# Longformer attention into a squared-ReLU expert layer: value rows picked on TensorE, casts and memsets on GpSimd, one unit of matmuls moved

## The chip, the cores and the metric

The kernel runs on one core of one Trainium2 chip. The metric is the device time of one execution in microseconds (us). The span in a profile is about 1.8 us shorter than that time.

## The reference

Attention with a window of 32 and eight global tokens is computed for 8 batches of 8 heads over 576 tokens with head size 64. Its output goes as 4608 rows of 512 into an expert layer.

```python
def _attn_ref(q, k, v, global_idx):              # q, k, v: (8, 8, 576, 64) float32
    scores = 1/np.sqrt(64) * np.matmul(q, k.transpose(0, 1, 3, 2))
    mask = np.abs(pos[:, None] - pos[None, :]) <= 32
    mask = mask | is_global[:, None] | is_global[None, :]       # 8 global tokens
    ...                                          # softmax over the masked scores
    return np.matmul(attn, v)

def _moe_ref(x, w_in, w_out):                    # x: (4608, 512), d_ff 2048
    r = np.maximum(x @ w_in, 0.0)
    return (r * r) @ w_out
```

## The kernel before

A batch has four pairs of heads. "Outputs" multiplies a pair's weights `et` with the values `vb`, and "finish" normalises the result into `xT`, the input of the expert layer. A "scatter" puts the eight rows of the global tokens into `xT` as eight small VectorE copies. Their column numbers were loaded into VectorE registers from SBUF beforehand. A "unit" is four expert matmuls of 512 columns, and `take(n)` emits n units of a queue between pieces of attention. `keep_warm(n)` emits n filler matmuls on a zero tile.

Batch 0 (start of the program, shortened):

```python
def fetch_globals():                      # SyncE: row numbers from a register
    for g in range(NG):                   # batch 0's eight value rows, one DMA each
        nc.sync.dma_start(out=gv0[g : g + 1], in_=v[0, :, ds(at[g], 1), :]...)
    for nm in "kqv": ...                  # rows of batches 1 and 2: 24 more DMAs

tr_k(3, ...)                              # last transposes of batch 0
keep_warm(4)                              # fillers
half0(2)                                  # scores and exp of pair 2
columns()                                 # clamp the row numbers
masked(0, ets[1], WIN)
load_columns(0)                           # VectorE register load of the scatter columns
...
half0(3)
dve.tensor_copy(out=gv16, in_=gv0)        # cast of the value rows
spread_values(0, dve.tensor_copy)         # five copies into vb[0]
masked(0, ets[2], WIN); masked(0, ets[3], WIN)
half0_out(0, "mm"); half0_out(1, "sc"); half0_out(2, "acc"); half0_out(3, "mm")
...
scatter(0, 0)                             # then the first expert matmuls may start
...                                       # second half of batch 0, its scatter, expert work
```

Batch 1 (shortened; `unit` computes one pair and takes expert units in three places):

```python
for hp in range(NHP):
    unit(NHP + hp, SCHED["b1"][hp], ...)  # b1 = ((3,1,3), (2,1,2), (2,1,3), (2,1,3))
    if hp == 0:
        tokens_to_scratch(2)              # GpSimd: tokens of batch 2 to a DRAM scratch
        values(2)                         # GpSimd: value tiles of batch 2
    elif hp == 1:
        next_in_place()                   # VectorE: casts of batch 2's global rows
        globals_to_scratch(2)             # SyncE: those rows to the scratch
        transposes(2)                     # SyncE: kb, qb <- scratch, transposed loads
        value_globals(2)
    elif hp == 2:
        gather(0)
```

The softmax here doesn't subtract the row's maximum and nothing guards it: scores larger than these inputs give would overflow.

## Time and profile before

| | kernel before |
|---|---|
| Time, three runs | 327.07 us median (326.74 to 327.49) |
| Span of the profiled execution | 326.7 us (this execution took 328.47 us) |
| TensorE busy | 97% |
| TensorE without a gap from | 70.00 us to the last rows |

A timeline line reads: start in us, duration in us, engine, source line, operation, output<-input, shapes, count, and in brackets the idle time of that engine just before it and what ended it. PE is TensorE, DVE is VectorE, ACT is ScalarE, POOL is GpSimd, and SPq is SyncE's queue of transfers. First come batch 2's transposed loads in SyncE's queue, then the second scatter on VectorE.

```profile
57.84 3.07 SPq L421 DMA_TRANSPOSE kb<-scr_k  x1
61.15 2.51 SPq L421 DMA_TRANSPOSE qb<-scr_q  x1
```

```profile
35.94 1.66 DVE L741 COPY xT<-gx 128x4 f16 x8
```

```profile
64.88 0.41 ACT L692 ACTIVATE rec<-sc 128x288 f32<-128x288 f32 x1 [2.80 <-PE acc L660]
```

The entries of the two transposed loads in the queue last 5.58 us together and end at 63.66. The data of `qb` landed later, at 66.39, by the landing records of the packed trace. The eight scatter copies take 1.66 us, about 0.2 each. The logarithm is the first of the last pair of batch 1.

### The profile page before, as it was taken

How to read it: one execution, taken by the hardware profiler on the slowest of the kernel's cores; microseconds unless marked ns; L12 is line 12 of the kernel's file. 1: busy time of each engine (PE TensorE's matmuls, PEld its weight loads, DVE VectorE, ACT ScalarE, POOL GpSimd, SP SyncE). 2: the span in 40 equal slices, each digit the busy share in tenths (PEclk: the TensorE clock that was granted, in tenths of full speed). 3: DMA queues.
4: the chain of work that ended last, by engine and by line, in shares of the span. 5: the costliest groups of instructions: out<-in, count | busy, mean ns of one | idle time of the engine just before them, and what ended most of it. 6: DMA issues, size and time to landing. Idle time of an engine off the chain costs nothing.

```text
span 326.7 us, 6942 instructions
## 1 busy us (share of the span) xinstructions
PE 316.8 (97%) x2432; PEld 164.5 (50%) x2432; DVE 228.9 (70%) x684; ACT 211.7 (65%) x416; POOL 106.6 (33%) x138
## 2 busy tenths in 40 slices
PE   7979999999999999999999999999999999999996
PEld 3646774445554455455444554555455544444444
DVE  8686888687878875987598758885888674323421
ACT  4677985469953995499549954995499636404600
POOL 9734556309800870089107800680000000000000
PEclk9999999999999999999999999999999999999999
DMA  8999999949994999399969994999910011011012
GB/s 192 177 204 183 180 181 156 169 137 107 144 138 147 67 147 167 125 91 135 136 148 89 151 138 122 109 148 107 142 66 0 34 46 51 2 69 59 2 53 76
DMA packets 148356, 37.55 MB, mean 115 GB/s; under 512 B 136298, under 2 KB 143842, under 8 KB 148322
## 3 DMA queue, kind: packets, MB, share of 16 engines
q0 software_dynamic: 105168, 17.93, 76.2%
q1 hardware_dynamic: 43008, 19.05, 30.2%
q8 instruction: 19, 0.31, 0.4%
q14 instruction: 15, 0.12, 0.1%
q10 hardware_dynamic: 146, 0.13, 0.1%
HBM read 37.31 MB, written 17.05 MB: 166 GB/s over the span
## 4 chain that ended last, share of the span: by engine, by line
PE 80%; DVE 7%; SPq 6%; ACT 2%; issue 2%; DMA 1%; DVEq 0%
PE mm L577 26%; PE mm L514 26%; PE tr L514 9%; PE tr L577 7%; SPq L365 4%; PE sc L669 3%; PE acc L669 3%; PE sc L617 2%; SPq L360 2%; PE acc L617 2%; DMA grows<-in_v_dram 1%; DVE xT L741 1%; PE mm L533 1%; DVE gt L545 1%; DVE et L633 1%
## 5 line engine op out<-in xcount | busy, mean ns | idle before, releaser
L577 PE MATMUL mm<-w_out,gt 128*128 128x512 f16 x448 | 104.4, 379 | 0.0
L514 PE MATMUL mm<-xT,w_in 128*128 128x512 f16 x384 | 90.8, 379 | 0.4 <-DVE xT L741 0.4
L577 PEld LDWEIGHTS <-gt 128*128 128x128 f16 x560 | 52.4, 98 | 58.6
L514 PEld LDWEIGHTS <-w_in 128*128 128x128 f16 x512 | 47.5, 98 | 53.6 <-issue 0.6
L519 ACT ACTIVATE rl<-mm 128x512 f16<-128x512 f32 x96 | 54.5, 599 | 26.9 <-PE mm L514 26.9
L520 DVE TENSOR_TENSOR gt<-rl 128x512 f16<-128x512 f16 x128 | 51.1, 422 | 16.8 <-ACT rl L519 15.5
L626 ACT ACTIVATE et<-sc 128x880 f16<-128x880 f32 (+1 forms) x32 | 29.0, 905 | 44.3 <-PE sc L617 44.3
L633 DVE TENSOR_TENSOR et<-et,mask 128x880 f16<-128x880 f16 (+1 forms) x64 | 38.8, 614 | 21.9 <-ACT et L626 21.7
L113 POOL DMA_DIRECT2D vb<-in_v_dram x40 | 41.1, 1571 | 9.4 <-DMA w_in<-in_moe_w_in_dram 8.3
L514 PE MATMUL tr<-xT,w_in 128*128 128x512 f16 x128 | 33.0, 380 | 0.0
L554 DVE COPY ot<-mm 128x512 f32<-128x512 f32 (+1 forms) x29 | 19.6, 677 | 17.7 <-PE mm L577 15.8
L626 ACT ACTIVATE et<-acc 128x880 f16<-128x880 f32 (+1 forms) x32 | 29.1, 909 | 1.5 <-PE acc L617 1.4
L722 DVE TENSOR_TENSOR xT<-sc,rec 64x288 f16<-64x288 f32 (+1 forms) x55 | 25.1, 456 | 6.9 <-ACT rec L693 6.2
L693 ACT ACTIVATE rec<-rec 128x288 f32<-128x288 f32 x64 | 28.3, 443 | 2.0
L722 DVE TENSOR_TENSOR xT<-acc,rec 64x288 f16<-64x288 f32 (+1 forms) x55 | 25.0, 455 | 4.0 <-ACT rec L693 1.1
L409 POOL DMA_DIRECT2D scr_k<-in_k_dram x30 | 26.6, 1104 | 2.8 <-issue 2.8
L692 ACT ACTIVATE rec<-sc 64x288 f32<-64x288 f32 (+1 forms) x55 | 22.4, 406 | 7.7 <-PE sc L669 4.2
L917 POOL COPY pin<-gsh 1x1 f32<-1x1 f32 x5 | 0.9, 177 | 81.1 <-DVE gsh L710 81.1
L669 PEld LDWEIGHTS <-vb 128*128 128x128 f16 x288 | 21.3, 98 | 11.7 <-issue 0.3
L409 POOL DMA_DIRECT2D scr_q<-in_q_dram x24 | 24.7, 1563 | 3.3 <-DMA w_out<-in_moe_w_out_dram 3.3
L577 PE MATMUL tr<-w_out,gt 128*128 128x512 f16 x112 | 25.3, 379 | 0.0
L692 ACT ACTIVATE rec<-acc 64x288 f32<-64x288 f32 (+1 forms) x55 | 22.2, 403 | 1.2 <-PE acc L660 0.4
(143 smaller groups left out, 303.7 us busy)
## 6 DMA issues: line engine op xcount, KB each, us to landing
out_dram<-ot SPq DMA_DIRECT2D x35, 256.0 KB
vb<-in_v_dram POOLq DMA_DIRECT2D x32, 120.0 KB, 11.3
scr_q<-in_q_dram POOLq DMA_DIRECT2D x24, 144.0 KB, 5.7
scr_k<-in_k_dram POOLq DMA_DIRECT2D x24, 120.0 KB, 4.9
w_in<-in_moe_w_in_dram POOLq DMA_DIRECT2D x4, 512.0 KB, 9.5
w_out<-in_moe_w_out_dram POOLq DMA_DIRECT2D x4, 512.0 KB, 11.4
natk<-in_k_dram POOLq DMA_DIRECT2D x3, 288.0 KB, 15.2
natq<-in_q_dram POOLq DMA_DIRECT2D x3, 288.0 KB, 16.0
```

The costliest lines, as they stand in the source:

```text
L113: pool.dma_start(out=vb[b][NG : NG + KN[x], x, 2 * hs.start : 2 * hs.stop : 2], in_=v[b, hs, x * KT : x * KT + KN[x]].rearrange("h s d -> ...
L409: pool.dma_start(out=scr[(nm, b % 2)][x * pitch + off : x * pitch + off + hi - lo].rearrange("s (h d) -> s h d", d=D), in_=src[nm][b, :, l ...
L514: nc.tensor.matmul(ph, w_in[:, t, u * P : (u + 1) * P], xT[:, t, XOFF + c * TC : XOFF + (c + 1) * TC], start=(t == 0), stop=(t == NDM - 1),)
L519: nc.scalar.activation(out=rl, in_=ph, func=AF.Relu)
L520: nc.vector.tensor_tensor(out=gts[c][:, u, :], in0=rl, in1=rl, op=ALU.mult)
L577: nc.tensor.matmul(po, gts[c][:, f, m * P : (m + 1) * P], w_out[:, f, :], start=(f == 0), stop=(f == NFF - 1),)
L626: act.activation(out=et[:, :, 0:W], in_=sc[:, :, 0:W], func=AF.Exp, bias=0.0, scale=scale)
L633: dve.tensor_tensor(out=et[:, :, 0:W], in0=et[:, :, 0:W], in1=mask[:, MB[half] : MB[half] + W].unsqueeze(1).to_broadcast((P, 2, W)), op=AL ...
L669: nc.tensor.matmul(banks[e][:, o : o + w], vtf[:, t, vo : vo + P], et[:, e, so : so + w], start=(n == 0), stop=(n == nw - 1), skip_group_c ...
L692: act.activation(out=rec[r], in_=av[xs][rs, :, 0:GTOK], func=AF.Ln)
L693: act.activation(out=rec, in_=rec, func=AF.Exp, scale=-1.0)
L722: dve.tensor_tensor(out=xT[r, hp, x0 : x0 + HS].rearrange("p (k x) -> p k x", k=2), in0=av[x][r, :, 0:GTOK], in1=rec[r], op=ALU.mult,)
```

## The change

The intent is to take work off VectorE and SyncE on the way to the first expert matmuls, and off VectorE in batch 1. Batch 0's value rows come from the value tiles, which are in SBUF anyway, by five one-hot products on TensorE. Batch 2's rows are cast on GpSimd in an idle stretch of it. The constant columns of `vb[0]` are set on GpSimd, and the index arithmetic moves. One unit moves from the last pair of batch 1 to the second. Batch 1 does 24 units in both kernels. The cut below leaves out that the mask of pair 1 comes earlier, that the fillers `w8` go, and that a tail of `vb[1]` is cleared on GpSimd instead of VectorE.

```diff
-SCHED = dict(... w6=4, ... w=2, ... b1=((3, 1, 3), (2, 1, 2), (2, 1, 3), (2, 1, 3)), ...)
+SCHED = dict(... w6=0, ... w=5, ... b1=((3, 1, 3), (2, 1, 3), (2, 1, 3), (2, 1, 2)), ...)
@@ fetch_globals
-        for g in range(NG):
-            nc.sync.dma_start(out=gv0[g : g + 1], in_=v[0, :, ds(at[g], 1), :]...)
@@ next_in_place
-            dve.tensor_copy(out=g16s[nm], in_=grow[nm][:, 1])
+            pool.tensor_copy(out=g16s[nm], in_=grow[nm][:, 1])
@@ new
+    def clear_value_rows():               # on ScalarE, at the very start
+        act.copy(out=vb[0][0:NG, :, 0 : 2 * H : 2], in_=idle[0:NG]...)
+    def pick_values():
+        gp = pst("mm", [P, 512])[0:NG]
+        for x in range(NT):
+            nc.tensor.matmul(gp..., oh[:, x, :], vb[0][:, x, 0 : 2 * H : 2],
+                start=(x == 0), stop=(x == NT - 1))
+        dve.tensor_copy(out=gv16, in_=gp...)
@@ batch 0
     keep_warm(SCHED["w6"])
+    pick_values()
+    spread_values(0, dve.tensor_copy)
     half0(2)
+    half0(3)
+    masked(0, ets[2], WIN)
+    masked(0, ets[3], WIN)
     columns()
     load_columns(0)                       # now behind the spreads and masks
 ...
+    next_in_place()                       # casts, right after the weight loads' issue
 ...
-    half0(3)
-    dve.tensor_copy(out=gv16, in_=gv0)
-    spread_values(0, dve.tensor_copy)
-    masked(0, ets[2], WIN)
-    masked(0, ets[3], WIN)
@@ batch 1, inside a pair
-                if i == NHP + 2:           # between the two output halves
-                    index_base()
-                    gather_index()
 ...
         elif hp == 2:
-            clear_ones(dve.memset, vb[0], range(0, 2))
+            index_base()
         elif hp == 3:
-            clear_ones(dve.memset, vb[0], range(2, NT))
+            gather_index()
@@ batch 1, after pair hp
         if hp == 0:
             values(2)
-        elif hp == 1:
-            next_in_place()
+            clear_ones(pool.memset, vb[0])
             globals_to_scratch(2)
             transposes(2)
+        elif hp == 1:
             value_globals(2)
-        elif hp == 2:
+        elif hp == 3:
             gather(0)
```

More of the change, by code (lines that the diff above doesn't have):

```diff
@@ L42 @@
 MB = (0, 456)
-SCHED = dict(w8=2, w9=3, w5=3, w6=4, w7=4, wa=4, wb=3, wc=3, g0=1, w0=2, w1=4, w2=2, w3=2, w4=3, w=2, h0=0, h1=3, h2=1, h3=0, keep=1, b1=((3, 1, 3), (2, 1, 2), (2, 1, 3), (2, 1, 3)), last=((2, 1, 4), (3, 1, 4), (2, 1, 4), (2, 1, 7)))
+SCHED = dict(w8=2, w9=3, w5=3, w6=0, w7=4, wa=4, wb=3, wc=3, g0=1, w0=2, w1=4, w2=2, w3=2, w4=3, w=5, h0=0, h1=3, h2=1, h3=0, keep=1, b1=((3, 1, 3), (2, 1, 3), (2, 1, 3), (2, 1, 2)), last=((2, 1, 4), (3, 1, 4), (2, 1, 4), (2, 1, 7)))
 ONES = 2.0**-7 * (1.0 + 15360.0 / 2**23)
@@ L347, in store_rows @@
         )
-    grows = sbt("grows", [NG, 7, H, D], FP32, bufs=2, tag="gt")
+    grows = sbt("grows", [NG, 6, H, D], FP32, bufs=2, tag="gt")
     grow = {nm: grows[:, 2 * i : 2 * i + 2] for i, nm in enumerate("kqv")}
-    gv0 = grows[:, 6]
     g16s = {nm: sbt("g16s" + nm, [NG, H, D], FP16) for nm in "kqv"}
@@ L358, in fetch_globals @@
         )
-        for g in range(NG):
-            nc.sync.dma_start(
-                out=gv0[g : g + 1], in_=v[0, :, ds(at[g], 1), :].rearrange("h o d -> o h d")
-            )
         for nm in "kqv":
@@ L443 @@
     gv16 = sbt("gv16", [NG, H, D], FP16)
+    def clear_value_rows():
+        act.copy(
+            out=vb[0][0:NG, :, 0 : 2 * H : 2],
+            in_=idle[0:NG].rearrange("p (h d) -> p h d", d=D).unsqueeze(1).to_broadcast((NG, NT, H, D)),
+        )
+    def pick_values():
+        gp = pst("mm", [P, 512])[0:NG]
+        for x in range(NT):
+            nc.tensor.matmul(
+                gp.rearrange("p (h d) -> p h d", d=D), oh[:, x, :], vb[0][:, x, 0 : 2 * H : 2],
+                start=(x == 0), stop=(x == NT - 1),
+            )
+        dve.tensor_copy(out=gv16, in_=gp.rearrange("p (h d) -> p h d", d=D))
     def spread_values(b, op, tiles=range(NT)):
@@ L752 @@
     bands()
+    clear_value_rows()
     keep_warm(SCHED["w0"])
@@ L787 @@
     masked(0, ets[0], WIN)
+    masked(0, ets[1], WIN)
     keep_warm(SCHED["w9"])
@@ L790 @@
     keep_warm(SCHED["w6"])
+    pick_values()
+    spread_values(0, dve.tensor_copy)
     half0(2)
-    clear_tail(dve.memset, vb[1])
+    half0(3)
+    masked(0, ets[2], WIN)
+    masked(0, ets[3], WIN)
     columns()
-    masked(0, ets[1], WIN)
     load_columns(0)
@@ L800 @@
             fetch_tokens(pool, nm, 1, i, 2)
+    clear_tail(pool.memset, vb[1])
     for x in range(NT):
@@ L804 @@
         pool.dma_start(out=w_out[:, ts(j, 4), :], in_=wo[:, ts(j, 4), :])
+    next_in_place()
     keep_warm(SCHED["w7"])
-    half0(3)
-    dve.tensor_copy(out=gv16, in_=gv0)
-    spread_values(0, dve.tensor_copy)
-    masked(0, ets[2], WIN)
-    masked(0, ets[3], WIN)
-    keep_warm(SCHED["w8"])
     half0_out(0, "mm")
```

## The prediction

> **What bounds the kernel now.** I read the page first: engine shares, then the chain that ended last, then the TensorE timeline stage by stage, and last the VectorE timeline around each TensorE gap.
>
> ```profile
> PE 316.8 (97%) x2432; PEld 164.5 (50%) x2432; DVE 228.9 (70%) x684; ACT 211.7 (65%) x416; POOL 106.6 (33%) x138
> PE 80%; DVE 7%; SPq 6%; ACT 2%; issue 2%; DMA 1%; DVEq 0%
> 160.00:200.00 40.00, 40.00 (x274) 20.18 (x269) 30.41 (x88) 28.70 (x56) 12.75 (x15) 1.00 1.36 136
> 60.00:70.00 10.00, 8.62 (x74) 3.95 (x71) 7.36 (x29) 5.10 (x8) 2.97 (x3) 1.00 0.84 172
> ```
>
> The first two lines are from the page (busy time, chain). The other two are stretches of the kernel: start:end, length, then busy us of TensorE, its weight loads, VectorE, ScalarE, GpSimd. From 70 us to the last rows TensorE has no gap, so the end time is the moment at which that saturated part begins (70.00) plus a constant. All that the change can win lies before 70 us. There the TensorE timeline shows these gaps (start, length, instruction, in brackets the idle time before it and its releaser):
>
> ```profile
> 13.72 1.04 PE L197 MATMUL tr<-idle 128*128 128x512 f16 x4
> 17.65 0.26 PE L660 MATMUL mm<-et,vb 128*64 128x160 f16 x2 [0.73 <-DVE vb L447]
> 25.09 1.03 PE L533 MATMUL mm<-xT,w_in 128*128 128x256 f16 x8 [1.52 <-DVE xT L741]
> 52.42 0.37 PE L617 MATMUL acc<-qt,kt 64*128 64x112 f16 x6 [0.24 <-DVE xT L722]
> 60.77 0.37 PE L617 MATMUL acc<-qt,kt 64*128 64x112 f16 x6 [0.66 <-DVE xT L722]
> 68.31 0.37 PE L617 MATMUL acc<-qb,kb 64*128 64x112 f16 x6 [0.36 <-DVE xT L722]
> 70.00 1.02 PE L514 MATMUL mm<-xT,w_in 128*128 128x512 f16 x4 [0.36 <-DVE xT L741]
> ```
>
> All real gaps end on VectorE. The first line is filler (warming matmuls on a zero tile); such fillers between 13.7 and 27 us hide further waiting, so the gap view alone understates it. VectorE between 14 and 24 us:
>
> ```profile
> 14.88 0.61 DVE L633 TENSOR_TENSOR et<-et,mask 128x912 f16<-128x912 f16 x1
> 16.86 0.41 DVE L807 CAST gv<-grows 8x512 f16<-8x512 f32 x1 [1.37 <-DMA grows<-in_k_dram]
> 17.31 1.51 DVE L447 COPY vb<-gv 8x512 f16<-8x512 f16 x5
> 18.74 1.16 DVE L633 TENSOR_TENSOR et<-et,mask 128x912 f16<-128x912 f16 x2
> 19.83 0.24 DVE L699 TENSOR_REDUCE gs<-mm 128x8 f32<-128x16 f32 x2
> 23.39 1.65 DVE L741 COPY xT<-gx 128x4 f16 x8
> L731 DVEq TENSOR_LOAD <-g32a x1: 835/835/835, 15.1 to 15.1; - x1
> ```
>
> So the first expert matmul (25.09) hangs on the scatter (23.39 to 25.04), that on the output finishing of four pairs (19.83 on), that on the spread of the global value rows, and that on the cast at 16.86. The 1.37 us before the cast are not all a DMA: the last line, from the instructions of that source line, is a register load of 0.835 us on VectorE's queue, inside the gap.
>
> **What the Trainium skill says.** (1) "TensorE: Matmul & The Clock Gate", Back-to-back issue gap: a lone 512-column matmul costs N/2.4 + 2.5, 216 ns. The trace agrees: four fillers end in 1.04 us, and groups of four run at 0.86 us apart. (2) "DMA: Bandwidth & Descriptors", Latency and other measured facts: a register load (tensor_load) costs some 600 ns at least. The trace has 0.835, 0.602 and 0.593 us for the three on VectorE. (3) "GPSIMD Engine Reference", 3.1: at best 1.8 cycles per element, 512 elements in 769 ns. Before has no such cast on GpSimd, so no run shows it yet. (4) "SBUF — State Buffer", Who interferes with whom: a VectorE instruction with two SBUF inputs contends with a GpSimd instruction that reads SBUF, exclusively. Before has no such pair to check it on.
>
> **The change, part by part.**
>
> *Value rows, TensorE.* The eight row fetches of v (SyncE queue, 6.54 us in all) go, and the other rows come that much earlier, though nobody on the path waits for them. In their place come five 8x512 products (5 x 0.216 = 1.08 us) right after the last batch 0 transposes, at 13.72, where four fillers (0.87 us) stood. They wait for all five value tiles. The fourth was issued at 6.9 and landed after 7.0 us (13.9); earlier tiles came 0.6 to 1.0 us apart, so the fifth comes at about 14.5 to 14.8 (estimate). The products end at about 14.9 to 15.1. Scores of pair 2 start then, against 14.69; those of pair 3 follow at once, at 15.3 against 15.98, as the fillers between move behind them.
>
> *Value rows, VectorE.* The copy out of PSUM (8x512; 0.62 us, the duration of the 128x512 output copy) runs 15.1 to 15.75, and the five spreads (5 x 0.21 spacing) to 16.85: before they ended at 18.82. Masks of pairs 2 and 3 (2 x 0.55) end at 18.0, against 19.9. But the register load moved behind them: index clamps to 18.35, load of 0.835 to 19.2. Only then the first reduction, 19.83 before. From there VectorE needs 23.39 - 19.83 - 0.15 (one wait for ScalarE) = 3.41 us, so the scatter starts at 22.65 instead of 23.39. **Gain 0.7 us**, not the 1.9 us that the spreads come earlier. TensorE is not the limit: five fillers instead of two before 25.09 (1.08 us) fit in a wait of 1.52 us plus fillers. In fillers 12 become 9, so TensorE's busy time changes by 1.08 - 0.65 = +0.4 us with no meaning for the end.
>
> *Clearing the value rows on ScalarE.* 8x2560 elements: from 96x768 in 0.83 us and 128x128 in 0.30 us, 0.83 ns an element, so 0.30 + 2432 x 0.00083 = 2.3 us, from 2.6 to 4.9 us. The next ScalarE cast waits for its DMA until 5.14: free, with 0.2 us to spare.
>
> *Batch 2's rows cast on GpSimd.* Three casts (0.84 + 0.40 + 0.71 on VectorE, 52.28 to 54.14) leave a VectorE stretch after which TensorE does not wait; on GpSimd 3 x 0.77 = 2.3 us (estimate from the skill) fall in the 2.10 us that GpSimd waited before 37.73. The store that waited 23.5 us for them, and the transposed loads at 57.84, come earlier; TensorE did not wait for these at 67.58.
>
> *Index arithmetic and constant columns.* Ten small operations (58.30 to 60.2) leave the place between the two output halves of pair 2 of batch 1. The xT write that TensorE waited for at 60.77 then ends near 59, so the **0.66 us** go. The memsets of ones (0.55 and 0.82 us) go to GpSimd, idle 5.78 us there.
>
> *Unit order.* Batch 1 still does 24 units, but one (four matmuls, 0.86 us) moves from behind pair 3 to behind pair 1: it covers the 0.24 us at 52.42 and takes cover away at the end:
>
> ```profile
> 64.88 2.76 PE L577 MATMUL mm<-w_out,gt 128*128 128x512 f16 x12
> 67.58 0.36 PE L617 MATMUL sc<-qb,kb 64*128 64x160 f16 x6
> 66.17 0.68 DVE L554 COPY ot<-mm 128x512 f32<-128x512 f32 x1
> ```
>
> The outputs of pair 3 end at 64.82, the saturated part begins 5.18 us later, after a VectorE chain (reduce, xT, ot copy, reduce, quotient, xT, scatter). With the units shifted, the ot copy (0.6 us spacing) falls before the outputs: 4.57 us. So outputs end at 64.82 - 0.7 - 0.24 - 0.66 + 0.86 = 64.08, and the saturated part begins at 68.65 instead of 70.00. **Sum: 1.35 us.** I take off 0.1 for GpSimd's interference: 327.07 - 1.25 = 325.8.
>
> **Rivals.** (a) *GpSimd blocks VectorE.* The casts at 35.7 to 38 meet the second scatter (35.94 to 37.55), squarings and masks, each with two SBUF inputs, and TensorE already waits 0.32 us for that scatter at 37.65. For it: the contention rule above. Against: filler-free matmuls follow that can be late by some tenths. Cost 0.3 to 0.8 us, time 326.1 to 326.6. (b) *The register load overlaps after all, or the finishing is bound by ScalarE* (0.79 us a pair from 17.4: 20.6, against 22.3 before): the front gains 1.5 us, time 325.0. (c) *The transfer binds.* Batch 1's q tokens, issued at 13.16, landed 16.0 us later, at 29.2; TensorE takes them at 31.32, about 30.6 after the change. Still early, but if the values landed late (the fifth at 15.5) the front gain is gone: 326.5. (d) *Tail uncovered:* if the ot copy does not leave the chain, the moved unit costs 0.6 us: 326.4.
>
> **Range and chances.** The terms are 0.7 (0.2 to 1.5) and 0.65 (0 to 0.9); together 0.1 to 2.4, so 324.7 to 327.0. Two per cent is 6.5 us, more than all the waiting before 70 us that can be removed (gaps of about 4.5 us after 16 us): faster 0.01, same 0.98, slower 0.01.
>
> **What would show it.** First reduction of pair 0 near 19.2 with the register load just before; first expert matmul near 24.4; no wait near 60; a longer wait, near 1 us, at batch 2's first scores; the first 512-column expert matmul near 68.7 and no gap after. It is wrong if the products end after 15.8, if VectorE operations beside the casts stretch to 0.8 us, or if the saturated part has gaps.

## The result

| | before | after |
|---|---|---|
| Median of 4 runs, us | 327.28 (326.74 to 327.94) | 327.53 (327.51 to 327.99) |
| Ratio after to before | | 1.001, 95% interval 0.9989 to 1.0032 |
| Span of the profiled execution | 326.7 | 325.7 |

A ratio in this document is the mean time of one kernel's fast runs over that of the other's in the same rounds. It is not quite the ratio of the medians.

327.5 lies outside the range of 324.7 to 327.0 and is 1.7 us above the 325.8 that was named. The two profiled spans mislead here. After's execution took its usual 327.51 us, while before's took 328.47, some 1.2 us above its own median.

The page of the changed kernel shows the same engine shares as before. The stretch of 60 to 70 us has 0.8 us more TensorE work than in before's profile (columns as in the prediction).

```profile
PE 316.4 (97%) x2434; PEld 164.4 (50%) x2434; DVE 227.9 (70%) x675; ACT 214.1 (66%) x417; POOL 110.0 (34%) x147
PE 85%; DVE 7%; DMA 2%; POOL 2%; ACT 2%; issue 1%; DVEq 0%; ACTq 0%; POOLq 0%
60.00:70.00 10.00, 9.45 (x82) 4.33 (x80) 7.83 (x27) 5.18 (x9) 2.97 (x3) 1.00 1.28 141
```

These are the waits of TensorE in the changed kernel.

```profile
14.91 0.38 PE L449 MATMUL mm<-vb,oh 128*8 128x512 f16 x1 [0.31 <-DMA vb<-in_v_dram]
19.97 0.26 PE L670 MATMUL mm<-et,one 128*64 128x160 f16 x2 [1.04 <-DVE gs L709]
25.10 1.03 PE L543 MATMUL mm<-xT,w_in 128*128 128x256 f16 x8 [1.02 <-DVE xT L751]
38.28 1.92 PE L543 MATMUL mm<-xT,w_in 128*128 128x256 f16 x16 [0.94 <-DVE xT L751]
67.40 0.37 PE L627 MATMUL sc<-qb,kb 64*128 64x160 f16 x6 [0.39 <-DVE xT L751]
69.09 1.02 PE L524 MATMUL mm<-xT,w_in 128*128 128x512 f16 x4 [0.16 <-DVE xT L751]
```

The waits near 52 and 60 us are gone, as predicted. The first expert matmul is at 25.10, where it was 25.09. A wait of 0.94 us stands at the second scatter, where it was 0.32. The saturated part begins at 69.09. On VectorE this is the path to the first expert matmul, then the second scatter, and last the register load, from the instructions of its source line.

```profile
15.33 0.68 DVE L453 CAST gv<-mm 8x512 f16<-8x512 f32 x1 [1.15 <-PE mm L449]
16.04 1.49 DVE L457 COPY vb<-gv 8x512 f16<-8x512 f16 x5
19.66 0.26 DVE L709 TENSOR_REDUCE gs<-mm 128x8 f32<-128x16 f32 x2 [0.89 <-PE mm L670]
23.00 2.04 DVE L751 COPY xT<-gx 128x4 f16 x8
35.94 2.28 DVE L751 COPY xT<-gx 128x4 f16 x8
```

```profile
L741 DVEq TENSOR_LOAD <-g32a x1: 839/839/839, 18.7 to 18.7; - x1
```

The cast is 1.5 us earlier than before. One of the five spread copies behind it, at 16.25, took 684 ns beside a GpSimd memset (16.13 to 16.78), the one of `vb[1]` that the change had moved there. In e10 and e13 below, where that memset ended before the spreads, each copy took 274 to 281 ns. Then the register load, from 18.74 to 19.58, stands right before the first reduction, although the bracket names TensorE. The reduction is only 0.17 us earlier than before. Both scatters are longer than the 1.65 and 1.66 us that they took before. GpSimd's timeline shows what ran beside them.

```profile
23.96 0.90 POOL L113 DMA_DIRECT2D vb<-in_v_dram  x1 [2.75 <-DMA w_in<-in_moe_w_in_dram]
...
35.38 0.60 POOL L370 CAST g16sk<-grows 8x512 f16<-8x512 f32 x1
35.94 0.64 POOL L370 CAST g16sq<-grows 8x512 f16<-8x512 f32 x1
36.53 0.60 POOL L370 CAST g16sv<-grows 8x512 f16<-8x512 f32 x1
...
50.71 4.42 POOL L113 DMA_DIRECT2D vb<-in_v_dram  x5 [0.58 <-PE acc L670]
```

In the first scatter one copy of the eight, at 24.27, took 564 ns instead of 177. In the second the copies at 36.15 and 36.65 took 459 and 522 ns. The last of these lines is the issue of batch 2's value loads. In SyncE's queue the transposed loads now follow those at once, and they last 12.6 us where they lasted 5.6.

```profile
52.27 5.37 SPq L416 DMA_TRANSPOSE kb<-scr_k  x1
57.93 7.22 SPq L416 DMA_TRANSPOSE qb<-scr_q  x1
```

`qb` landed at 67.23 in this execution, and TensorE's wait ended at 67.40, although the bracket there names VectorE. So it was a wait for `qb`. In e2, e3 and e5 below `qb` landed at 68.28, 67.81 and 68.40, and TensorE went on at 68.41, 67.94 and 68.54.

### The profile page after: what moved, and what is told of

Its sections match the earlier page's. It is cut to its first block, busy times and chain, and to the rows that moved or that the text cites. A ratio compares the mean times of both kernels' runs of the same rounds, so it can differ in the third digit from the quotient of the medians.

```text
span 325.7 us, 6920 instructions
## 1 busy us (share of the span) xinstructions
PE 316.4 (97%) x2434; PEld 164.4 (50%) x2434; DVE 227.9 (70%) x675; ACT 214.1 (66%) x417; POOL 110.0 (34%) x147
## 4 chain that ended last, share of the span: by engine, by line
PE 85%; DVE 7%; DMA 2%; POOL 2%; ACT 2%; issue 1%; DVEq 0%; ACTq 0%; POOLq 0%
PE mm L587 28%; PE mm L524 26%; PE tr L524 9%; PE tr L587 7%; PE sc L679 3%; PE acc L679 3%; PE sc L627 2%; DMA vb<-in_v_dram 2%; PE mm L543 2%; DVE xT L751 2%; PE acc L627 1%; POOL vb L113 1%; DVE et L643 1%; DVE xT L732 1%; ACT et L636 1%
## 5 line engine op out<-in xcount | busy, mean ns | idle before, releaser
L587 PEld LDWEIGHTS <-gt 128*128 128x128 f16 x560 | 52.4, 98 | 58.6
```

What stands on the lines that cost most here:

```text
L587: nc.tensor.matmul(po, gts[c][:, f, m * P : (m + 1) * P], w_out[:, f, :], start=(f == 0), stop=(f == NFF - 1),)
```

## The experiments

My theory is that four things ate the gain.

- **Register load:** it moved onto the path.
- **GpSimd casts:** they stretch the second scatter.
- **Value loads:** those of batch 2 make the earlier transposed loads slow.
- **Moved unit:** it leaves the last scatter uncovered.

One rival is that the products themselves, or the transfer of the value tiles, set the front. Another is that nothing was lost and the differences are noise. Each table gives the median of the run, the median of the kernel before in the same rounds, and the ratio with its 95% interval.

### Noise: the two kernels again, unedited

> The kernel before, unchanged, against itself. Theory B (the profile that I predicted from was one of its slow executions; run-to-run time of this kernel varies by over 1 us because descriptor writing on GpSimd collides, or not, with VectorE copies): the spread of single times is about 1.2 us again, and a second profile with another total differs at the scatters (1.65 us when free, about 2.0 when hit) or the spread of the value rows. Theory A (before is steady at 326.7 to 327.1 and the first profiled run was an outlier of the profiler): spread under 0.5 us and the same gaps on TensorE.

> The changed kernel, unchanged, on the same chip as e1. If the true change is the 1.0 us that the two traces show, the ratio is 0.997 (about -1.0 us); if the change truly is nothing, 1.000 to 1.001. In the trace the second scatter of batch 0 is again 2.2 to 2.4 us long (the casts on GpSimd always meet it), while the first one is 1.65 or about 2.0 depending on when the weights land.

| run | us | before, us | ratio |
|---|---|---|---|
| e1_same_before | 328.31 (327.08 to 330.45) | 327.31 | 1.0039 (1.0009 to 1.0070) |
| e2_same_after | 327.28 (326.62 to 328.25) | 327.31 | 0.9992 (0.9970 to 1.0014) |

The kernel before, against itself, came out 0.4% slower with an interval that leaves out 1. So a ratio here tells nothing below about 0.5% by itself, and the experiments below are read by their traces first. In e2 the two scatters took 1.91 and 2.24 us, and TensorE was saturated from 69.77, in an execution of 328.25 us. In e1 both scatters took 1.65 us, so it was not the collisions named in theory B that set the two traces of the kernel before apart. The trace of e1 also corrects the baseline. TensorE's wait near 60 us, the start of the saturated part and the late logarithm read:

```profile
60.47 0.37 PE L617 MATMUL acc<-qt,kt 64*128 64x112 f16 x6 [0.37 <-DVE xT L722]
68.63 1.03 PE L514 MATMUL mm<-xT,w_in 128*128 128x512 f16 x4
```

```profile
63.21 0.41 ACT L692 ACTIVATE rec<-sc 128x288 f32<-128x288 f32 x1 [1.37 <-PE sc L660]
```

The logarithm started at 63.21 instead of 64.88, and TensorE had no wait after it: the saturated part began at 68.63, not at 70.00. The profile that the prediction was built on was of an execution slower than the median. Why ScalarE started that logarithm late there stays open. No edit of the kernel aimed at it.

### e3: the register load early, alone

```diff
+    columns()
+    load_columns(0)
     pick_values()
 ...
     masked(0, ets[3], WIN)
-    columns()
-    load_columns(0)
```

> The changed kernel with the index clamps and the register load put back ahead of the value rows, where VectorE idles 1.15 us. Theory T1 (the register load, 0.84 us, stands on the path between masks and first reduction): the first reduction moves from 19.66 to about 18.7, TensorE's 1.04 us wait in the outputs of pair 3 goes, the first scatter starts at about 22.2 and the time falls by 0.5 to 0.9 us against e2. Rival T2 (the front is bound elsewhere, by ScalarE's logarithms or by the scatter's collision): the time falls by less than 0.3 us.

Measured: 327.69 against 327.31, ratio 1.0007 (0.9983 to 1.0031). The register load ran at 14.3, and these are TensorE's waits and the second scatter.

```profile
23.63 1.03 PE L543 MATMUL mm<-xT,w_in 128*128 128x256 f16 x8 [0.86 <-DVE xT L751]
37.44 1.92 PE L543 MATMUL mm<-xT,w_in 128*128 128x256 f16 x16 [1.57 <-DVE xT L751]
67.94 0.37 PE L627 MATMUL sc<-qb,kb 64*128 64x160 f16 x6 [1.75 <-DMA qb<-scr_q]
```

```profile
34.47 2.91 DVE L751 COPY xT<-gx 128x4 f16 x8
```

The first expert matmul came 1.47 us earlier than in the changed kernel, so the register load theory is shown. The other traces agree: with the load late and a start at the usual time (after, e2, e4, e5, e8) that matmul comes at 24.54 to 25.29, with it early (e3, e6, e7, e9, e12) at 23.60 to 23.77. The load itself is 0.84 us of that, and 0.39 us is the first scatter, which took 1.65 us here as it had moved away from GpSimd's issue. The time did not move, because the gain was lost twice. The second scatter came 1.5 us earlier and met the GpSimd casts, which had not moved (35.41 to 37.13), so it took 2.91 us. Then TensorE waited 1.75 us for `qb`, whose loads did not come earlier.

### e4 and e5: the casts elsewhere

e4 leaves the casts on GpSimd and moves them behind the second scatter. e5 puts them back on VectorE, one pair later, with the stores and the transposed loads.

```diff
 # e4
-    next_in_place()                       # before keep_warm(w7)
 ...
     pool.tensor_copy(out=pin[0:1], in_=xT...)      # waits for the second scatter
+    next_in_place()
 # e5
-            pool.tensor_copy(out=g16s[nm], in_=grow[nm][:, 1])
+            dve.tensor_copy(out=g16s[nm], in_=grow[nm][:, 1])
 ...
-            globals_to_scratch(2)          # at hp == 0
-            transposes(2)
         elif hp == 1:
+            next_in_place()
+            globals_to_scratch(2)
+            transposes(2)
             value_globals(2)
```

> The changed kernel with the three GpSimd casts issued after the pin that waits for the second scatter, so that they can't meet it. Theory T3 (the casts' reads block the scatter's copies): the second scatter falls from 2.28 to 1.65 us, the TensorE wait at its end from 0.94 to about 0.3, and the time falls by 0.6 us against e2; squarings and masks right after may stretch instead. Rival: the scatter is slow for another reason (a descriptor write) and stays at 2.0 to 2.3; time as e2.

> The changed kernel with one part undone: the three casts of batch 2's rows are on VectorE again, at the end of pair 1 of batch 1, with the row stores and the transposed loads behind them as before. Theory Q (the early casts release the transposed loads of batch 2 at 52 us, into the value loads; there they take 12.9 us instead of 5.8, end at 65 to 66 us instead of 63.7, and TensorE waits for qb at batch 2's first scores): the transposed loads start near 57.8, take about 3.1 and 2.6 us, qb is there by 66, TensorE has no wait at the scores, the second scatter is 1.65 us again, and the time falls by 0.6 to 1.5 us against the changed kernel (ratio to before 0.994 to 0.998). Rival T3 (only the scatter's collision matters, e4 was noise): 0.6 us at the scatter, and the wait at the scores stays near 1 us.

| run | us | before, us | ratio | second scatter | TensorE's wait for it |
|---|---|---|---|---|---|
| e4 | 327.92 | 327.31 | 1.0016 (0.9994 to 1.0038) | 1.65 us | 0.32 us |
| e5 | 327.85 | 327.37 | 1.0024 (0.9993 to 1.0055) | 1.65 us | 0.31 us |

The theory of the GpSimd casts is shown: without casts beside it the second scatter is as short as before. In e4 the casts then met two masks on VectorE, the pair of two-input operations that the prediction's point (4) had no case of: the masks took 1.97 us together instead of 1.14. Two of the casts took 0.99 us each instead of 0.60, and TensorE waited again a little later (GpSimd, then TensorE):

```profile
38.27 0.99 POOL L370 CAST g16sq<-grows 8x512 f16<-8x512 f32 x1
39.21 0.99 POOL L370 CAST g16sv<-grows 8x512 f16<-8x512 f32 x1
```

```profile
40.40 0.26 PE L670 MATMUL sc<-et,vb 128*64 128x160 f16 x2 [0.58 <-DVE vb L457]
```

In e5 the transposed loads were short again (2.86 and 2.84 us). They started only at 60.01, some 2 us later than in the kernel before, and TensorE waited 2.13 us at batch 2's first scores. That part of e5's expectation missed. It shows the other horn: late and short loads land no earlier than early and long ones (`qb` at 68.40 here, in an execution of 329.99 us, and at 67.23 in the changed kernel).

### e6: e3 and e5 together

> e3 and e5 together. Theory Q: the 1.4 us that e3 won at the front (first expert matmul at 23.6 instead of 25.1) and lost to the wait for qb (1.75 us) now stays: batch 2's saturated part begins near 67 us and the time is 325 to 326, ratio to before 0.992 to 0.996, unless qb is again too late for the earlier TensorE, then a wait of at most 0.5 us. Rival (the front gain is lost in another wait): time as e5.

Measured: 327.19, ratio 1.0000 (0.9975 to 1.0025), span of the profiled execution 324.9. The first expert matmul was at 23.77 and the second scatter's wait was 0.41. New waits stood at 55.04 (0.57 us, for a mask on VectorE, which did the casts just before) and at 66.93 (1.02 us, batch 2's first scores). The traces add up as the parts do. The times still do not show it.

### e8 and e7: what slows the transposed loads

e8 is wrong: it is the changed kernel without batch 2's value loads, with a relative error of 0.44. e7 gives correct results: e3 and e4 together, with the value loads held until `kb` has landed.

```diff
 # e8
-            values(2)
 # e7, at hp == 0, besides the edits of e3 and e4
-            values(2)
-            clear_ones(pool.memset, vb[0])
             globals_to_scratch(2)
             transposes(2)
+            clear_ones(pool.memset, vb[0])
+            pool.tensor_copy(out=pin[0:1], in_=kb[2][0:1, 0, 0:1])   # waits for kb
+            values(2)
```

> Wrong on purpose: the changed kernel without batch 2's value loads (it uses batch 0's), to see the transposed loads without them. Theory Q: kb and qb take about 3 us each from 52 us, over by 60, no wait at batch 2's scores. Rival: they take over 5 us each as in the changed kernel.

> e3 and e4 together, and batch 2's value loads issued only when kb is there, so that the early transposed loads run without them. Theory Q: kb takes about 3 us and qb up to 5, both are there before 62 us, no wait at the scores; the value loads land by about 66 to 68, before TensorE's outputs of batch 2 at about 69 need them. Time 325 to 326. Rival (the transposed loads are slow in that stretch because of the token stores, not the values): they still take over 5 us each.

e8 took 326.91 us in its one run, whose state is unknown, and e7 327.55 (326.69 to 328.32), ratio 1.0008 (0.9982 to 1.0034). SyncE's queue of e8, then of e7:

```profile
51.59 3.86 SPq L416 DMA_TRANSPOSE kb<-scr_k  x1
55.74 3.36 SPq L416 DMA_TRANSPOSE qb<-scr_q  x1
```

```profile
51.47 3.86 SPq L416 DMA_TRANSPOSE kb<-scr_k  x1
55.61 3.25 SPq L416 DMA_TRANSPOSE qb<-scr_q  x1
```

Without value loads beside them the transposed loads take 7.2 us instead of 12.6 and end near 59. TensorE has no wait at batch 2's first scores in either trace. So the value loads cause 5.4 us of the 7.0 us by which these loads were longer than before. The other 1.6 us stay open: the token stores that precede them are a rival that no run took away. The Trainium skill says it in general ("DMA: Bandwidth & Descriptors", Issuing engines are not separate DMA queues): transfers of all issuing engines interleave on the same 16 DMA engines. Loads issued by GpSimd stretched loads issued by SyncE from 7.2 to 12.6 us.

### e9, e10, e12: a repaired version

e9 joins the repairs. The register load is early. The three casts run on VectorE in three stretches where it is idle (near 26.5, 27.8 and 30.4 us). The value loads follow `kb`, and the units are in before's order. e10 is the same with the moved unit, and e12 is e10 once more.

```diff
+    columns(); load_columns(0)            # before pick_values()
-            pool.tensor_copy(out=g16s[nm], in_=grow[nm][:, 1])
+            dve.tensor_copy(out=g16s[nm], in_=grow[nm][:, 1])
-    next_in_place()
+    next_in_place("k")                    # after half1_out(0)
+    next_in_place("q")                    # after half1_out(1)
+    next_in_place("v")                    # after take(h1)
 # value loads behind kb as in e7; e9 only: b1 as in the kernel before
```

> The changed kernel with the row-number load ahead of the value rows, batch 2's three casts on VectorE in three stretches in which it is idle, batch 2's value loads held until kb has landed, and the units in the kernel before's order. Theory (the change's gain was eaten by the register load, by value loads beside the transposed loads, by GpSimd beside the second scatter and by the uncovered last scatter): first expert matmul near 23.6 us, second scatter 1.65 us, no wait of TensorE for qb, last scatter covered; TensorE saturated from 66.8 to 67.3, span 323.5 to 324, time 325.2 to 325.8, ratio to the kernel before 0.994 to 0.996. Rival (the casts on VectorE delay the pairs' outputs, or a new wait takes the place of the removed ones): span 325 to 326 and ratio 0.999 to 1.001, as every run so far.

> As e9_best, but with the change's order of units (three of batch 1 per pair). Theory: the moved unit leaves the last scatter uncovered, so TensorE waits 0.5 to 0.8 us at the start of its saturated part, and the span is 0.3 to 0.5 us longer than that of e9_best. Rival: the moved unit fills a wait in the middle of the same size (near 52 or 60 us) and the spans agree within 0.2 us.

> The same kernel as e10_best_moved_unit, once more. Identical copies of the kernel before differed by 0.4% with an interval that left out 1, so one interval does not settle 1 us. If the gain of e10 (ratio 0.9952) is real: ratio 0.994 to 0.997 again, spans 324.2 to 324.6 in most executions. If it was a lucky set: ratio 0.998 to 1.001.

| run | us | before, us | ratio |
|---|---|---|---|
| e9 | 326.81 (326.43 to 327.67) | 327.67 | 0.9977 (0.9952 to 1.0001) |
| e10 | 326.38 (326.09 to 327.02) | 327.67 | 0.9952 (0.9929 to 0.9975) |
| e12, same kernel as e10 | 326.16 (325.89 to 327.68) | 327.18 | 0.9973 (0.9941 to 1.0004) |

TensorE's waits in e12, and its last scatter on VectorE:

```profile
23.74 1.03 PE L543 MATMUL mm<-xT,w_in 128*128 128x256 f16 x8 [0.87 <-DVE xT L751]
36.37 1.92 PE L543 MATMUL mm<-xT,w_in 128*128 128x256 f16 x16 [0.39 <-DVE xT L751]
67.46 1.02 PE L524 MATMUL mm<-xT,w_in 128*128 128x512 f16 x4 [0.81 <-DVE xT L751]
```

```profile
65.29 2.12 DVE L751 COPY xT<-gx 128x4 f16 x8
```

The saturated part begins at 67.46 instead of 69.09, and the span is 324.0. Over e10 and e12 together the mean is 326.48 us of 12 runs, against 327.70 of 22 runs of the kernel before: 1.2 us, or 0.4%. That is as large as the difference that e1 showed between identical kernels. What speaks for a real gain is that two sets show it in one direction, and that the traces show the waits gone. The size, about 1 us, is uncertain.

e9's time lay above the 325.2 to 325.8 that was expected. Its saturated part began at 67.19, as expected, but then paused once: the value loads now come late.

```profile
70.13 0.41 PE L679 MATMUL acc<-et,vb 128*128 128x136 f16 x4 [0.53 <-DMA vb<-in_v_dram]
```

The expected lead of e9 over e10 did not show: e10 is ahead by 0.4 us, which is within the noise. So the theory of the moved unit is not borne out as I put it. The moved unit did leave the last scatter uncovered (0.81 us in e12, as e4, e7 and e8 had shown 0.51, 0.77 and 0.52). In the repaired version, however, it also fills e9's wait of 0.24 us at 51.27, and no wait for the late value loads appears in the trace of e10 or e12. The profile of e10 fell on its slowest execution (327.02), whose second fillers came at 3.47 instead of 2.43 and whose first expert matmul came at 25.14, so I read e12. e12's last scatter took 2.12 us, where it took 1.66 in both traces of the kernel before. GpSimd issued a gather from 65.08 to 66.13, beside it. Some 0.5 us may still be had there; that was not tried.

### e11: only the register load early, in the kernel before

```diff
     tr_k(1, ...)
+    columns()
+    load_columns(0)
 ...
-    columns()
 ...
-    load_columns(0)
```

> The kernel before with only the register load of the scatter columns moved ahead, to where VectorE is idle near 10.3 us. If most of the wait ahead of the cast of the value rows (16.86 us) was that register load: cast at 15.5 to 15.8 us, first expert matmul at 24.2 to 24.5 instead of 25.09, without any of the change. If it was the transfer of the value rows, as the profile names it: cast still at 16.7 to 16.9 and the expert matmul where it was, within 0.3 us. Time in both cases within 0.4% of the kernel before.

Measured: 328.58 (326.75 to 330.13), ratio 1.0013 (0.9975 to 1.0052), so nothing by the time. The profile fell on an execution whose TensorE sped up late. These are the fillers on TensorE, then VectorE's last copy of the transposes and the cast.

```profile
7.40 1.03 PE L197 MATMUL tr<-idle 128*128 128x512 f16 x2
8.88 1.46 PE L197 MATMUL tr<-idle 128*128 128x512 f16 x3
```

```profile
15.49 0.66 DVE L481 COPY kt<-mm 128x480 f16<-128x480 f16 x1 [0.92 <-PE mm L469]
...
17.38 0.41 DVE L807 CAST gv<-grows 8x512 f16<-8x512 f32 x1
```

In the first trace of the kernel before the pair of fillers at 7.27 took 0.60 us and that copy ran at 13.38. Here the copy is 2.1 us later, and the whole front with it, so the absolute times that were expected cannot be read. Relative to that copy, the cast came after 1.89 us instead of 3.48, and with no wait ahead of it. That does not separate the register load from the DMA that the profile names: SyncE's queue was not late (it issued the eight rows from 3.6 to 10.2, as before), so the rows had the 2.1 us more to land in. The next run separates them.

### e13: the repaired version with the value rows loaded as before

This undoes the change's first part alone: no products and no clear, but eight small transfers.

```diff
-    clear_value_rows()
-    pick_values()
+    dve.tensor_copy(out=gv16, in_=gv0)
 # fetch_globals loads gv0 again, ahead of the other rows; w6=4
```

> As e10_best_moved_unit, but with the change's first part undone: the eight value rows come by eight small transfers as in the kernel before, and are cast from what these bring; no products, no clear. Theory (the wait ahead of the cast was mostly the register load, which is moved ahead here, and only 0.4 to 0.5 us of it the transfers): cast at 15.6 to 16.2 us instead of 15.4, first expert matmul 0.1 to 0.6 us later than in an e10 execution with the usual start, time within 0.5 us of e10's. Rival (the transfers are what the cast waited for): cast at 16.7 to 17 us, expert matmul near 25, time 1 to 1.3 us above e10's.

Measured: 332.27 (332.05 to 334.11), ratio 1.0152 (1.0120 to 1.0184). The cast was at 15.72 and the first expert matmul at 23.55, so at the front the products are worth nothing once the register load is out of the way. The same eight transfers had landed by 15.72 at the latest, so of the wait of 1.37 us that ended at 16.86 in the kernel before they explain 0.2 us at most. The register load, from 15.1 to 16.0, covers some 0.5 us of that wait. From its end to the cast it is 0.46 us in e13 and 0.89 in the kernel before. What held the cast there for the other 0.4 us stays open. This half was close to what was expected. The time was not, by either theory: it is 5.9 us above e10's. TensorE, VectorE and SyncE's queue show why.

```profile
35.67 0.30 PE L675 MATMUL sc<-et,vb 128*64 128x112 f16 x2 [4.50 <-DVE et L648]
```

```profile
34.68 0.42 DVE L375 CAST g16sv<-grows 8x512 f16<-8x512 f32 x1 [4.33 <-DMA scr_k<-idle]
```

```profile
22.83 5.40 SPq L365 DMA_DIRECT2D grows<-in_v_dram  x8
```

The eight extra transfers take 6.55 us of SyncE's queue, so the last rows are issued until 28.2 instead of 22.0 (e12). The early cast on VectorE then waits until 34.68, and a mask and TensorE wait behind it. Without the products these casts would have to stand later; that was not run. Their place is what the products buy in this arrangement.

## Why the prediction was wrong

Three steps failed: the gain at the front, the early transposed loads taken as free, and the stretch before the saturated part, which was read from one slower execution. A fourth, GpSimd's block, was foreseen and given too little weight.

**The bound was right.** TensorE has no gap from the start of the saturated part on: 253.3 us remained in after, 253.4 in e1 and 253.3 in e12. The end follows the start of that part.

**The baseline was wrong.** The sum was taken off a median time, while its terms were read in one execution that was 1.4 us slower (328.47 against 327.07). Against e1, whose saturated part began at 68.63, the changed kernel's 69.09 is 0.46 later, not 1.35 earlier. The step that failed here is "the saturated part begins at 68.65 instead of 70.00". The stretch from the outputs to the saturated part was to shrink from 5.18 to 4.57. Counted from the first expert matmul behind the outputs, it is 5.12 in the trace used, 3.97 in after, but 4.06 already in e1. One execution is compared with one here, but both are near their kernel's median (327.51 and 327.08).

**"Gain 0.7 us" at the front became 0.** The reduction was named for 19.2 and came at 19.66. The fifth product waited for its tile until 14.91 and then took 0.38 us alone, where the sum had 0.216. The spreads took 1.49 us instead of 1.1, although the prediction's own line has 1.51 for them before: one copy fell beside the moved memset, which no run tested by itself. The register load followed as foreseen. The scatter at 23.00 was 0.39 earlier than before, but one copy beside GpSimd's issue of a value load stretched it by 0.39 us. The register load was known and still left on the path. Moving it is worth 1.47 us of front (e3), with what it spares the scatter.

**The middle was right.** The waits at 52.4 and 60.8 went. The second was 0.66 in the trace used, but 0.37 in e1's.

**Rival (a) was right and its weight wrong.** The GpSimd casts met the second scatter and cost 0.62 us (0.94 instead of 0.32). That lies in the 0.3 to 0.8 that rival (a) gave, but only 0.1 us was taken off for it. e4, e5 and e6 show that the casts are the cause. The mechanism was named only in part. In the changed kernel the casts met no squaring or mask, and the scatter's copies have one input each, so the rule on two inputs that the prediction cites does not cover them.

**"TensorE did not wait for these" failed.** The early transposed loads were treated as free. They now fall into batch 2's value loads, last 12.6 us instead of 5.6, and `qb` lands at 67.23 instead of 66.39 (65.84 in e1). TensorE waits 0.39 us for them in one execution and 1.25 in e2. e7 and e8 show the cause. The prediction's signs had a wait near 1 us at this place without saying for what; that one came there, for `qb`, is luck.

With the three repairs of e12, in which the moved unit stayed, the saturated part begins at 67.46, which is 1.2 us before e1's. That is close to the sum of 1.25, but by other parts: the front alone came 1.35 us earlier than in e1 (23.74 against 25.09), and casts and value loads stand elsewhere than in the change. So the agreement is in part luck, and the sum was wrong as what the change gives as it stands. None of the three things by which the prediction said that it would be wrong came about; they did not cover the steps that failed. The chances held, since 2% is 6.5 us.

## What to carry to other kernels

Take the baseline of a prediction from an execution at the median time, or from two traces: here one profile was slower than the median by as much as the change could win. When a transfer is released earlier, look at what it now runs beside, and when work moves to an idle engine, look at which short operations of its neighbour lie in that stretch. A register load on a vector engine's queue does not show as busy time and hides behind another name in the waits, so look for it by its own line and place it where the engine is idle.

## What the Trainium skill lacked or had wrong

- "DMA: Bandwidth & Descriptors", Latency and other measured facts, gives about 600 ns as the floor of a register load. The first on VectorE took 835 to 848 ns in the traces of before, after, e3, e11 and e12, and the two later ones 593 to 604 ns. The page does not mention the longer first one.
- "DMA: Bandwidth & Descriptors", Issuing engines are not separate DMA queues, agrees in direction but has no figure for a transposed load beside plain loads: 12.6 to 13.7 us beside value loads, 7.1 to 7.2 without them (e7, e8).
- "SBUF — State Buffer", Who interferes with whom, says that a copy in a two-port mode can be blocked by GpSimd for a whole instruction. It has no size for copies as small as the scatter's. Copies of 128x4 half-precision elements went from 177 ns to between 454 and 564 ns beside GpSimd's casts or its issue of a load, and a scatter of eight from 1.65 to as much as 2.91 us.
- "GPSIMD Engine Reference", 3.1, gives 769 ns for 512 elements at best. The casts of 8x512 from float32 to half precision took 0.60 to 0.64 us, less than that, and 0.99 us beside VectorE work (e4). Spans on GpSimd are rough in this profile.
- "TensorE: Matmul & The Clock Gate", What you observe, has the full speed come some 4 us into the activity, within half a microsecond from run to run; the section after it adds that the number of slow matmuls differs from run to run. The spread here is wider than half a microsecond, with the same TensorE work until then: the pairs of fillers fell from 1.03 us to 0.60 as early as 4.6 us (e3, first filler at 1.2), while in e11 fillers still ran at the slow rate until 10.3 us. The front of e11 was 2.1 us late.
